# Normalising row blocks on GpSimd instead of VectorE in a four-layer attention kernel

## The chip, the cores and the metric

The kernel runs on one core of a Trainium2 chip. The metric is the device time of one execution in microseconds; of before there are three runs, 420.8 to 422.5, median 421.62. The five engines of the core work through queues of their own: PE (TensorE, matrix products), DVE (VectorE), ACT (ScalarE), POOL (GpSimd) and SP (SyncE, here only a queue of DMAs). Each engine takes its instructions in the order in which they stand, and waits on semaphores for those of the others.

## The reference

Four residual blocks over x of 2048 rows and 512 columns in bf16, with 32 heads of 16 columns; A and B each have one set of weights that is used twice.

```python
def _A_ref(x, wqkv, wo):                       # linear attention
    q, k, v = split(x @ wqkv)
    phi = lambda t: jnp.where(t > 0, t + 1, jnp.exp(t)) + 1e-6
    pq, pk = phi(q), phi(k)
    kv = jnp.einsum("bhsd,bhse->bhde", pk, v)  # a sum over all rows
    z = jnp.einsum("bhsd->bhd", pk)
    ...
    return merge(num / den) @ wo

def _B_ref(x, wqkv, wo):                       # softmax over a window of 256 rows
    ...

x = x + _A_ref(_layernorm(x), A_wqkv, A_wo)
x = x + _B_ref(_layernorm(x), B_wqkv, B_wo)
x = x + _A_ref(_layernorm(x), A_wqkv, A_wo)
x = x + _B_ref(_layernorm(x), B_wqkv, B_wo)
```

`_layernorm` takes the mean and variance of each row, subtracts the mean and divides by the root of the variance plus 1e-5. It has no weights. The kernel calls the last step, `(x - mean) * rstd`, on one block of 128 rows a normalising.

## The kernel before, in words

The 2048 rows are 16 blocks of 128, one row on each partition. x stays in SBUF throughout (`xres`, 16 tiles of 128 x 512 bf16). There are four normalisings per block, 64 in all:

- `1.ln`: before the keys and values of the first A layer. These are summed over all blocks (`kv`), so nothing that needs the sum starts before the last block.
- `2.b.ln`: before the first B layer. In segment 2 a block runs through the rest of the first A layer (`a_q`, `a_out`, `wo`, which updates `xres`), then through B (`b_qkv`, `b_attn`).
- `2k.ln`: before the keys and values of the second A layer, a block at a time as B finishes it; again they are summed over all blocks, in `kvacc`.
- `3.b.ln`: before the second B layer, in segment 3, which is as segment 2 with the output at the end.

One normalising is five operations (`ln`, L809 on): `st` and `ag` on DVE (L814, L815: statistics, mean and variance), `ae` on DVE (L817: adds 1e-5), `rs` on POOL (L818: to the power -0.5, one element per row), `xn` (L820: the normalised block, 128 x 512, from SBUF to SBUF). Then `xT` transposes the block: by a DMA that SP issues (L828), or for a few blocks by PE (L835) and a copy. The projections of PE read `xT`.

What else the text speaks of: phi of q and k is an exponential on ACT (L879), a clamp on DVE (`E`, L880) and an addition on DVE (L883; L885 for some). The attention of B is scores on PE (L1007, L1056), exponentials on ACT of 128 x 1024 (L1035, L1077: `pH`, `pF`), masks on DVE that multiply in SBUF (L1043, L1095), products with the values on PE (L1113, L1125), division on DVE (L1135, L1137). The values reach their place through a copy (`vt`, L845) and DMAs that POOL issues (`vd`, L981, four a block). Copies out of PSUM (`qc`, `kb`, `vc`, and others) may stand on ACT or on DVE.

The order of the work is written out as a list: `graph` records 2764 operations, each with the engines that can run it and a cost for each, and `ORDER` is a list of their numbers in the order in which they are issued. A mark behind a number (`445'`) takes the second engine of the operation; figures behind a colon name the buffers. `_Sched.schedule` walks this list; what it puts on one engine stays in that order on the chip, and `emit` sets the waits. The costs only give the walk its times; the chip doesn't see them.

Of the kernel before, what the change touches and what calls it, by code (L numbers as in the profile page):

```python
# [9 lines left out]
ALU = mybir.AluOpType  # L10
# [337 lines left out]
658' 671 626 627 672 673 902:6 907:2 684 903 986:0.4.1 987 988 919 449:0 904 955 905:3 881:1 906:3 882:3 883 921:0.6.0 922 923 908 909 685 686:2 687:1 450:5  # L348
884 1407 960:3.0.3 451 961 910:2 911 677:2.1.5 678 912:2 989 962 1408 924 1409 452 474:6.0 475 476 488 477 478:2 479:3 937:3 938 679 933:0.4.1 934 935 674:2.1
675 700 701 1410 932 939 940:1 720 964:0.6.2 702 703 965 966 688:5.0 689 690 691 1411:3 936 942:4 1412:0 941:1 489:0.3 490 943 501 676' 1021:2.6.2 1022 944  # L350
1023 704:0 491 492 493:0 494:1 705:3 967 692:5.2 693 945:2 946 947:0 680 963 721 694' 956:0.2.0 957 958 954 480:4 481 482 644 645 662 1418:7.1 995:0.5.4 996
997 722:1 723:2 1419 1420' 990 913:4 914 915 968:0.2.5 969 970 495:7 496 713:6.2.0 714 715 959 503 497 504:0.0 505 999:4.2.1 1000 1001 972:7 971 977:6 506 973
507 508:3 1056:0.4.0 1057 1058 1024 736 737 974 975:1 738 976:2 978 979 991:0.2.0 992 980:3 981 1421 1422 1423 998 710:7.3 711 712' 993 706:6.1 707 708' 709'
1030:0.4.3 681 716 1031 1032 695:3.1.1 696 994 948:2 1002 1003:0.6.2 697' 1004 949 950 1435 509:3 982:2 510:5 983:4 984 1005 1006 663 1034:0.2.5 1035 985 1036
511 1012:7 512 772 1436 1437 739 1438 740:2 741:4 1060 1007:6 1008 1439:3 1440:2 1424 1449 1450 1091:0.4.1 1092 754 1093 513:3.12.1 514 515 1013 1014 1009
1010:2 1451 517 1011:0 1026:0.4.0 1027 1028 728:2.0 1015:0 1016 1413:3.1.0 1414 1415 729 755 1425:0 1426:1 698 1037 1065:0.6.1 1066 730' 1416 1417 1067
731:5.0.3 732 724:4.2 733 725 1038:0.2.2 1039 1040 1441:7.0.2 1446:6.0 1447 1442 1029 1025 1033 1042:5 1443 1069:0.2.4 1070 1071 726' 1095 1043 727'
1427:4.4.3 1428 1429 699 1452 1448' 1453:1 1041 1047:6 1044 1126:0.2.2 1127 756 1444 1445 1068 746:7.1 747 1017:1 1045:1 1454:5 1046:1 1128 1430 1431 1048
1094 1061:0.4.0 1062 1063 1049 748' 1050:3 1051 757 1052:0 758:2 759:0 1018:3 1019 1100:0.6.3 1101 1102 1020 1465 1466 1467 1460:2.4 773 774 1455:5.3.0 1456
1073:0.3.5 1103 1461 1074 1457 1462 1432:7.3 742:6.3 1433 743 1075 775 1072 1059 1064 1077:2 1078 744 1458 1459 1104:0.4.2 1105 1106 1076 1434' 1079 1082:3  # L360
1083 745' 1080:2 1081:3 516 717 1161:0.6.0 1162 1163 1084 1085:0 764:2.2 765 1086 518 1087:2 766' 1096:0.4.0 1097 1098 1130 749:3.1.2 750 767:2.2.4 776:3 1107
1165 1135:0.6.1 1136 751' 1137 768 769' 1053:5 777:3 1054 1108:0.3.4 1099 1055 1479 760:2.4 761 762' 1468 1109 1110 1111 734 1112:7 1139:0.5.5 1140 1141 1113
1114 763' 1115:1 770 1469:0 1117:4 1118 1116:2 752 1196:0.2.1 519:5.3 1129 520 1197 521 522 1198 523:0 524:3 1119 1120:2 543:7.13.2 544 545 1480 1121 547
1088:1 1199 1131:2.5.0 1142 1089 1090 782:4.3 783 1164 1493 1132 1133 1134 528:7.14.3 1138 1170:0.2.3 1171 784' 1172 529 530 532 778:6.5 779 780' 781' 525:5
526 1143:0.2.2 753 1144 1145 527 790 791 735 1147:4 1148 792 1122:1 1494 1149 1150:0 1146 1151:1 1174:0.6.4 1175 793 1176 794:1 546 1470:3 1476:5.2 1477
1471:3.2.0 1478' 1177 1472 1473 1474 1475 1152:4 1153 1231:0.6.2 1232 1233 1481 531 1482 1154 1155:1 1156 1123:5 533 1124 1166:0.2.0 1125 1507 1173 558:4.15.1
# [72 lines left out]
class _Kernel:  # L439
# [369 lines left out]
    def ln(self, n, t, ring, dma=True):  # L809
        s = self.s  # L810
        x = self.xres[t]
# [7 lines left out]
        xn = self.r_xn.buf()  # L819
# [549 lines left out]
```

## Time and profile before

| | before |
|---|---|
| median of three runs | 421.62 us |
| lowest, highest | 420.8, 422.5 us |
| the profiled execution's own time | 422.47 us |
| its span in the profile | 421.1 us |
| PE, DVE, ACT, POOL busy | 392.3, 382.3, 383.6, 106.0 us |
| normalisings (L820), all on DVE | 64, 25.8 us |

Busy times are unions of the profiled durations. A duration on DVE or ACT includes the run-out of the instruction, in which the next one can already start. A row of a group reads: line, engine, operation, tiles written and read, shape and type, count, then busy us, mean ns of one, idle us of the engine just before them and what ended it. In the chain that ended last the columns are the start, the length booked on the chain, engine, tile and line.

### The profile page before, as it was taken

The numbers are of one execution on the slowest core, as the hardware profiler recorded it, in microseconds if no ns is written. First come the engines' busy times: TensorE is split into PE (matmuls) and PEld (weight loads), VectorE is DVE, ScalarE is ACT, GpSimd is POOL, SyncE is SP. The second block draws the span as 40 slices with busy tenths as digits, with TensorE's granted clock in tenths as the row PEclk, the third lists the DMA queues.
The fourth block names the chain that finished last, engine by engine and source line by source line (L and its number), as shares of the span: only waits on it lengthen the run. The fifth ranks groups of instructions, "written<-read, shape, count | busy, mean of one in ns | idle before, by whom it ended". The sixth has DMA issues, their size and how long they took to land.

```text
span 421.1 us, 18887 instructions
## 1 busy us (share of the span) xinstructions
PE 392.3 (93%) x8330; PEld 284.2 (67%) x8404; DVE 382.3 (91%) x1003; ACT 383.6 (91%) x496; POOL 106.0 (25%) x202
## 2 busy tenths in 40 slices
PE   7999989999999899998999999998999899988997
PEld 3655766776766676767586667676767667666675
DVE  7999899999999899998999899999999999978774
ACT  4888679999999999999899767899999999999995
POOL 2230024225232231423131100332322212605200
PEclk9999999999999999999999999999999999999999
DMA  8334426314252130523141201324415422406143
GB/s 265 112 64 138 128 55 126 66 41 99 41 68 43 38 67 16 85 41 59 39 80 22 48 9 39 70 48 68 79 34 80 60 52 33 90 16 117 43 103 92
DMA packets 75720, 29.22 MB, mean 69 GB/s; under 512 B 65264, under 2 KB 73584, under 8 KB 75632
## 3 DMA queue, kind: packets, MB, share of 16 engines
q1 hardware_dynamic: 70336, 22.36, 26.4%
q0 software_dynamic: 4096, 4.46, 5.7%
q8 instruction: 68, 1.11, 1.1%
q10 hardware_dynamic: 1200, 1.11, 0.9%
q14 instruction: 20, 0.16, 0.1%
HBM read 6.29 MB, written 2.10 MB: 20 GB/s over the span
## 4 chain that ended last, share of the span: by engine, by line
PE 42%; ACT 33%; DVE 18%; issue 3%; DMA 3%; POOL 0%; DVEq 0%
ACT pF L1077 23%; PE ps L858 16%; PE ps L870 8%; ACT pH L1035 6%; PE ps L1125 6%; PE ps L1056 5%; PE ps L1113 3%; DVE stats L814 2%; DVE o L954 2%; ACT kbd L971 2%; DMA w_Av<-in_A_wqkv_dram 2%; DVE pF L1095 1%; DVE xres L893 1%; PE ps L916 1%; PE ps L1007 1%
## 5 line engine op out<-in xcount | busy, mean ns | idle before, releaser
L1077 ACT ACTIVATE pF<-ps 128x1024 bf16<-128x1024 f32 x240 | 229.4, 1085 | 4.4 <-PE ps L1056 2.6
L818 POOL TENSOR_TENSOR rstd<-mv,const 128x1 f32<-128x1 f32 x64 | 39.1, 617 | 241.6 <-DVE mv L817 238.6
L981 POOL DMA_DIRECT2D vbd<-vt x128 | 67.1, 532 | 48.2 <-DVE vt L845 30.6
L1035 ACT ACTIVATE pH<-ps 128x1024 bf16<-128x1024 f32 (+1 forms) x64 | 60.3, 1022 | 3.5 <-PE ps L1007 3.2
L1125 PE MATMUL ps<-vbd,pF 128*128 128x34 bf16 x1856 | 60.2, 178 | 2.4 <-issue 2.4
L1125 PEld LDWEIGHTS ps<-vbd,pF 128*128 128x128 bf16 x1856 | 53.3, 96 | 5.5 <-issue 2.7
L1056 PE MATMUL ps<-qT,kbd 32*128 32x128 bf16 x1920 | 48.5, 216 | 5.0 <-ACT pF L1077 2.1
L1095 DVE TENSOR_TENSOR pF<-pF,const 128x512 bf16<-128x512 bf16 (+2 forms) x116 | 46.6, 415 | 3.6 <-ACT pF L1077 3.5
L879 ACT ACTIVATE E<-ps 128x512 bf16<-128x512 f32 x64 | 40.1, 630 | 9.8 <-PE ps L870 6.4
L814 DVE BATCH_NORM_STATS2 stats<-xres 128x6 f32<-128x512 bf16 x64 | 44.0, 689 | 2.0 <-DMA xres<-in_A_x_dram 1.1
L1056 PEld LDWEIGHTS ps<-qT,kbd 32*128 32x128 bf16 x1920 | 28.5, 92 | 22.6 <-ACT pF L1077 9.6
L1043 DVE TENSOR_TENSOR pH<-pH,const 128x1024 bf16<-128x1024 bf16 (+1 forms) x64 | 41.1, 649 | 0.0
L870 PE MATMUL ps<-xT,w_Bq 128*128 128x128 bf16 x512 | 35.5, 219 | 1.0 <-ACT pF L1077 0.7
L870 PE MATMUL ps<-xT,w_Bk 128*128 128x128 bf16 x512 | 35.6, 219 | 0.6 <-ACT pF L1077 0.4
L1113 PEld LDWEIGHTS ps<-vbd,pH 128*128 128x128 bf16 x928 | 29.0, 96 | 8.3 <-issue 2.2
L870 PE MATMUL ps<-xTa,w_Aq 128*128 128x128 bf16 x512 | 34.2, 219 | 0.3 <-DVE pq L883 0.2
L858 PE MATMUL ps<-w_Ak,xTa 128*128 128x512 bf16 (+2 forms) x121 | 32.3, 372 | 1.6 <-issue 0.8
L858 PE MATMUL ps<-w_Av,xTa 128*128 128x512 bf16 (+1 forms) x128 | 32.7, 371 | 1.1 <-issue 0.5
L1113 PE MATMUL ps<-vbd,pH 128*128 128x34 bf16 x928 | 32.7, 178 | 0.9 <-DVE kbd L971 0.3
L858 PE MATMUL ps<-w_Ao,oT 128*128 128x512 bf16 (+2 forms) x119 | 29.4, 354 | 4.2 <-issue 1.6
L870 PEld LDWEIGHTS ps<-xT,w_Bk 128*128 128x128 bf16 x512 | 29.8, 98 | 5.0 <-issue 0.9
L870 PEld LDWEIGHTS ps<-xT,w_Bq 128*128 128x128 bf16 x512 | 29.5, 98 | 5.3 <-issue 2.0
(96 smaller groups left out, 625.6 us busy)
## 6 DMA issues: line engine op xcount, KB each, us to landing
vbd<-vt POOLq DMA_DIRECT2D x128, 34.0 KB, 2.4
xres<-in_A_x_dram SPq DMA_DIRECT2D x16, 128.0 KB, 5.7
out_dram<-xres SPq DMA_DIRECT2D x15, 128.0 KB, 2.3
oT<-o SPq DMA_TRANSPOSE x60, 2.8
w_Ak<-in_A_wqkv_dram ACTq DMA_DIRECT2D x1, 512.0 KB, 5.4
w_Av<-in_A_wqkv_dram ACTq DMA_DIRECT2D x1, 512.0 KB, 6.9
w_Aq<-in_A_wqkv_dram SPq DMA_DIRECT2D x1, 512.0 KB, 7.0
w_Ao<-in_A_wo_dram SPq DMA_DIRECT2D x1, 512.0 KB, 3.9
```

The costliest lines, as they stand in the source:

```text
L814: s.op(n + ".st", {"DVE": 0.595}, lambda e, en: e.bn_stats(a_st, x.h[:]), reads=[x], writes=[st])
L858: i = e.matmul(g.h[:, a:b], xT.h[:, kt, :], w.h[:, kt, a:b], start=(kt == 0), stop=(kt == 3), skip_group_check=True)
L870: i = e.matmul(g.h[:, f * P:(f + 1) * P], w.h[:, kt, f * P:(f + 1) * P], xT.h[:, kt, :], start=(f == 0 and kt == 0), stop=(kt == 3), skip_ ...
L879: s.op(n + ".e", {"ACT": _act_cost(512)}, lambda e, en: e.activation(E.h[:], g.h, ACT.Exp, bias=0.0), reads=[g], writes=[E])
L981: return [e.dma_start(vbd.h[64 * a:64 * a + 64, j, a], vt.h[64 * j:64 * j + 64, a]) for j in range(2)]
L1035: return e.activation(d, c, ACT.Exp, bias=0.0, scale=DH ** -0.5)
L1043: return e.tensor_tensor(v, v, tr, ALU.mult)
L1056: i = e.matmul(ss[r // 2].h[:, r % 2, k * P:k * P + P], kbds[fj[m] // 2].h[32 * r:32 * r + 32, f, fj[m] % 2, :], qT.h[32 * r:32 * r + 32, ...
L1077: s.op("e%d%d" % (u, g), {"ACT": _act_cost(1024)}, lambda e, en, S=ss[g], pb=pb, g=g: e.activation(pb.h[:, 2 * g:2 * g + 2, :], S.h, ACT.E ...
L1095: return e.tensor_tensor(v, v, tr, ALU.mult)
L1113: i = e.matmul(U.h[:, c:c + 34], pH.h[:, 4 * r + f, 64 * a:64 * a + P], vbds[j // 2].h[:, j % 2, :, 4 * f + r, :], start=first[0], stop=Tr ...
L1125: i = e.matmul(U.h[:, c:c + 34], pFs[at[f, m][0]].h[:, r, at[f, m][1] * P:at[f, m][1] * P + P], vbds[fj[m] // 2].h[:, fj[m] % 2, :, 4 * f ...
```

## The change

`xn` may run on POOL, and the order list is replaced by another. In the new list 51 of the 64 `xn` carry the mark for POOL; 13 stay on DVE.

```diff
 def ln(self, n, t, ring, dma=True):
...
         s.op(n + ".rs", {"POOL": 0.53}, lambda e, en: e.tensor_tensor(a_rs, v, self.half.h[:], ALU.pow), reads=[mv, self.half], writes=[rs])
         xn = self.r_xn.buf()
-        s.op(n + ".xn", {"DVE": 0.32}, lambda e, en: e.tensor_scalar(xn.h[:], x.h[:], self.mv[:, t, 0:1], a_rs, op0=ALU.subtract, op1=ALU.mult),
+        s.op(n + ".xn", {"DVE": 0.32, "POOL": 0.7}, lambda e, en: e.tensor_scalar(xn.h[:], x.h[:], self.mv[:, t, 0:1], a_rs, op0=ALU.subtract, op1=ALU.mult),
              reads=[x, mv, rs], writes=[xn], new=[xn])
...
 ORDER = """
-37 4 0 3 6 7 1 8 9 2 68 61:7 69 70 5 67 71 72:0 73:6.0 62 38 66 85 86 87 10 39 40 88 41 42 43 44 45 46 11 33 12 13 20 47 89:1 22 74 75:7.0.0 76 90:6.1 81:5.0
+1 67 3 2 4 0 6 7 8 9 37 68 5 69 70 39 40 61:7 38 66 41 71 72:0 73:6.0 85 86 87 42 43 44 45 46 33 10 74 62 75:7.0.0 76 11 12 13 88 22 89:1 90:6.1 25 91 32 102
...
```

Counted in the two lists:

| | before | after |
|---|---|---|
| `xn` on DVE: `1.ln`, `2.b.ln`, `2k.ln`, `3.b.ln` | 16, 16, 16, 16 | 3, 4, 4, 2 |
| `xn` on POOL | 0, 0, 0, 0 | 13, 12, 12, 14 |
| `kb` of segments 2 and 3 on ACT, DVE | 25, 39 | 26, 38 |
| `qc` on ACT, DVE | 8, 24 | 7, 25 |
| `vc` of segments 2 and 3 on ACT, DVE | 9, 23 | 8, 24 |
| `vc` of `1` on ACT, DVE | 10, 6 | 9, 7 |
| `vc` of `2k` on ACT, DVE | 6, 10 | 10, 6 |
| `zc` of the last block on ACT, DVE | 3, 1 | 2, 2 |

All other operations stay on their engines. Their order changes on every engine; which block's transposition runs on PE or by DMA does not.

More of the change, by code (lines that the diff above doesn't have):

```diff
@@ L348 @@
[L348 to L355, printed above, removed]
@@ new lines @@
+352 353 109:6.2.1 110 186 205 206':1 187 188 126:7.3.2 127 130 116 149:3.3 150 157':2 173 174':3 189 26 219 52 367 111 128 266 190':0 220 53 282 283 117
+143:2.4.3 129 158:1.5 18 159 144 145 131 366 221 368 222:2 267 268 151 269 207:6 132:7.4 133 112 270':1 147 101 166:1.5 167 284 408:0.3.2 54 55 250 251 113
+114 252 253 134 168' 409 412 214:6.6 215 410 208:7.5.0 209 212 210 285 146 160:3.6.1 161 162 148 234 235 236 27 164 28 163 211 213 165 175:7 176:2.7.3 177 118
+180 182:7.7 135 183 178 191:8 192:3.0.0 193 223:9 29 23 152 230:2.0 198:1.1 231 194 411 196 413 179 232 314 315 316 181 271:10 278:0.2 279 272:3.1.1 273 274
@@ new lines @@
+1407 988 921:0.3.0 922 923 908 1408 449:1 450:7 451 452 960:0.5.3 961 686':1 687:0 924 909 910:1 911 912:2 962 677:4.1.5 678 679 474:0.0 475 476 937:7 477
+478:3 479:3 1409 933:2.5.1 934 935 989 963 1410 1411':3 938 674:4.1 939 940:3 941:0 936 964:0.2.2 965 675 489:5.2 490 688:7.0 689 966 676' 942:4 491 492 943
+493:1 700 701 690 691 702 1021:0.2.2 944 480:5 481 1022 1023 945:1 946 703 704:0 956:0.6.0 957 482 955 692:4.2 693 913:5 995:0.2.4 694' 958 996 914 1412:1
+1418:4.6 1419 736 737 738 968:0.6.5 997 969 915 1420' 959 494:0 495:5 496 504:2.0 505 705:3 990 970 713:4.0.0 714 715 497 999:0.6.1 1000 1001 644 645 972:5
@@ new lines @@
+973 506 971 967 680 681 977:4 974 507 508:2 1056:0.2.0 754 1057 1058 739 740':2 1421 978 755 979 706:7.1 975:3 976:3 980:2 981 991:0.5.0 992 1002 707 708' 993
+710:4.3 711 709' 1030:0.2.3 1422 1031 1032 721 722':1 712' 947:1 948:6 949 756 950 1435 695:7.2.1 1003:0.4.2 1004 982:3 1005 696 697' 509:2 983:6 984
+1034:0.2.5 1035 510:7 1036 1423 1424 1436 511 1437 994 1438 998 1007:5 1006 1012:4 1013 723:2 985 512 772 1449 1037 1450 1091:0.2.1 1014 1015:1 1439':3 1440:0
+513:7.12.1 514 1008 1092 1024 1451 1009 1025 1093 515 1010:0 516 517 716 717 1026:0.2.1 1027 698 1425':0 728:6.0 729 1413:7.5.2 1011:1 1016 1017:0 1426:2
@@ new lines @@
+1065:0.4.2 1452 1453:1 1028 741:4 1414 1066 1067 730' 724:3.2 725 731:6.1.3 732 1415 1038:0.4.0 1059 1454:5 1446:2.0 1447 1095 733 726' 727' 773 1416 1029
+1417 1441:3.2.3 1448' 2718 1039 1040 1442 1443 1069:0.6.4 1070 1071 699 1033 1041 1444 1445 757 1427:2.6.0 1428 1042:5 1047:4 1060 1043 1044 1045:3 1046:0 734
+1429 1126:0.6.2 1127 1048 1430 1128 1049 1431 1050:2 1051 1052:1 1072 746:5.1 1061:0.2.1 747 1062 1063 1018:4 1019 518 748' 1100:0.6.3 1101 1020 1465 1130
+1432:5.5 1102 1064 1068 758':3 759:1 1433 1434 1460:4.4 1461 1073:0.2.5 1462' 742:7.3 774 743 744' 745' 1074 1077:6 1075 1076 1104:0.4.0 1078 1079 1080:0 1105
@@ new lines @@
+1106 1455:7.4.2 1456 1082:3 1129 1466 1467 1468 1469':0 1081:3 1457 1458 1161:0.4.0 1162 1163 1459 764:2.2 1107 1083 735 1084 1096:0.6.1 1097 1098 1085:1 1086
+765 766' 1103 749:5.0.2 750 751' 1135:0.3.2 1136 1137 767:2.2.4 1087:3 1094 768 1053:7 769' 1108:0.5.4 1109 1054 1099 760:4.4 1110 761 1055 762' 1139:0.2.5
+1140 1141 1111 775 1112:7 763' 1113 1114 1115:3 1117:6 519:0.2 1116:2 520 521 522 523:1 1196:4.2.1 543:7.13.3 544 770 1479 1197 1199 1198 547 545 1118
+1131:0.4.1 1119 1164 1120:0 1121 1088:3 1132 1133 1138 1089 1090 1493 776':2 1480 777:3 778:7.5 779 528:6.14.0 780 781' 529 532 1165 530 782:5.3 1170:0.2.3
@@ new lines @@
+783 784' 1494 1134 524:2 525:7 526 527 790 1171 1172 1495 791 792 1142 1470:3 531 533 1143:0.4.0 1144 1145 1146 752 753 793 794:1 1471:6.1.1 1472 1147:7
+1174:0.2.4 1175 1176 1148 1149 1150:1 1476:5.2 1477 1473 1152:4 1153 1478 1231:0.2.2 1232 1233 1474 1475 1154 1151:0 1155:3 1156 1122:0 1123:5 546 1124 1125
+1507 1496 1497':3 1166:0.6.1 785:4.1.5 786 787' 1167 1168 1508 558:5.15.2 559 562 560 534:0.2 535 536 537 538:3 1205:2.6.2 795:0 548 1169 1206 1207 796:4.0
+797 798' 800:5.0 1173 1178:0.2.5 1179 1180 801 803:7.0.1 1481 1177 799' 1182:6 1183 1184 1200 1209:0.2.0 1210 1211 804 1181 1187:4 1188 1185:0 1186:1 802'
@@ new lines @@
+856' 1662:3.2.2 1663 1664 1666 1321 1349:4.6.5 1350 1317 1521:1.0 1304 852' 853' 1322:2 861 1323 1324 1340 1522 1695 1348 1351 1352 1341:0.4.1 1697 1325:3
+1326:2 1327:3 1328 1329 1342 1343 1353:0.6.3 1330:2 1331 1344 1354 1543:2.4.3 1297:0 1298:5 1569':0 1299 1300 1581 1785 1355 1371:0.3.0 1372 1374 1373 1544
+1545 843 1357:7 1582 1562:6.5 1356 1358 1563 1564 1359 1583 1584 1585':2 1360:0 1361:1 1380:0.4.0 1381 1382 1332:1 1546 1547 1375 1665 1362:3 1363 1364 1365:1
+1366 1384:0.6.2 1385 1737:2.4.1 1333:5 1667 1386 1334 1383 1335 1595 1596 1376:0.3.1 1377 1378 1597 1379 1738 1557:7.5.3 1558 1570:11 1571:6.6.2 1572 1559
@@ new lines @@
+1941 2253:7 2254 2271 2249:0.4.4 2250 2251 1766 2255 2256:2 1973:3.1.0 2257:3 1974 2273:0.6.5 2274 2275 1955:2.2.2 1997 1998 1975' 2252 2222:5 2223 2224
+2277:0.3.0 2278 2279 1956 2272 2225:1 2226 2284 2258:7 2259 1957' 1982':3 2304:0.5.2 1983:0 1988:2.1 1989 1778:3 2305 2260 2306 2276 2014 1990' 1984:4.3
+2261:3 2317:0.2.3 2318 2319 2262 2280 1788:5.0 1789 1790 1791 1792:1 1779:7 1780 1781 1985 2320 1986 1987 1803:0.2 1804 1999 1805 65 2227:0 1806 2285:5.2.2
+2286 1958 1807:2 2228:7 2229 2230 2287 1991:4.0.3 1992 2308 1993' 2309:0.5.4 2310 2311 1959 2289:7 2288 2195:1 2000':1 2290 2291 2292:1 2293:0 2313:0.2.5 2314
@@ new lines @@
+2565:0.6.1 2566 2567 2142 2143 2336:5 2548 2528 2559 2337 2564 2338 2605:0.3.3 2549:0 2606 2607 2144':1 2145:4 2541:7 2542 2592:5.0.1 2593 2594 2543 2544:1
+2117:3.2.5 2545:1 2568 2550 2118 2551:3 2572 2443:2 2573:4.6.2 2574 2119' 2577:2 2578 2579 2580:3 2581:2 2575 2597:0.4.5 2138 2598 2599 2595 2128:3.5 2129
+2130' 2153:2.0.1 2139 2601:0.6.4 2602 2603 2154 2146:5.0 2147 2576 2131' 2628:0.3.2 2629 2630 2155' 2148' 2149' 2480:2 2481 2482 2641:6.0.1 2582:5 2642 2643
+2120 2121 2632 2600 2583 2604 2584 2585:2 2586 2609:2.6.0 2610 2611 2150:4.2 2151 2596 2152' 2162':0 2163:0 2171:5.1.2 2633:0.2.2 2634 2608 2635 2172 2173'
@@ L431 @@
+2612 2613:4 2614 2637:6.0.5 2638 2587:0 2639 2615 2616:1 2617:0 2444:5 2445 2446 2644 2447 2664:2.6.0 2168:4.3 2169 2636 2665 2666 2170' 2631 2618:5
[4 rows of a table added]
+2714:0.2 2716 2715:2 2725:2 2717 2730:5 2731 2732 2726:7.2 2733:1 2734 2727' 2696:6 2748:1 2749 2735:5.0 2750 2697 2743 2744:7.1 2720:4 2719:0 2339 2736 2728
+2737 2751:0 2729 2752 2753:5.3 2591 2745' 2738 2747 2754 2746 2755 2757 2756 2760 2761 2698 2699 2758 2627 2762 2759 2763
 """
```

92 lines of the change are left out of this document (34 added, 58 removed), and 63 rows, old and new, of the table ORDER.

## The prediction

> **What bounds the kernel now.** I read the page first (busy time of each engine, then the chain that ended last), then the busy time by stretch, then the chain through the middle.
>
> ```profile
> span 421.1 us, 18887 instructions
> ...
> PE 392.3 (93%) x8330; PEld 284.2 (67%) x8404; DVE 382.3 (91%) x1003; ACT 383.6 (91%) x496; POOL 106.0 (25%) x202
> ...
> PE 42%; ACT 33%; DVE 18%; issue 3%; DMA 3%; POOL 0%; DVEq 0%
> ```
>
> Three engines are over 90% busy and GpSimd (POOL) is at 25%. So no single engine bounds the span; each stretch has its own limit. The next view gives busy us (and instruction counts) by stretch. I set the cuts from the chain: 45.5 is where the first key-value sum is in, 60.5 the first attention exponential of the second segment, 225 roughly its last tile, 267 the first exponential of the third segment, 404.8 the last but for the tail.
>
> ```profile
> core 0: us, PE busy (x) PEld busy (x) DVE busy (x) ACT busy (x) POOL busy (x), PEclk, DMA share, GB/s
> 0.00:45.50 45.50, 43.02 (x309) 23.98 (x314) 38.75 (x135) 34.10 (x61) 10.01 (x26) 1.00 0.53 157
> 45.50:60.50 15.00, 13.17 (x179) 9.96 (x178) 14.12 (x44) 11.09 (x19) 2.19 (x4) 1.00 0.20 39
> 60.50:106.00 45.50, 42.46 (x925) 31.71 (x938) 43.65 (x113) 44.59 (x58) 16.67 (x31) 1.00 0.41 83
> 106.00:225.00 119.00, 112.27 (x2628) 83.57 (x2654) 111.10 (x277) 114.46 (x140) 31.26 (x56) 1.00 0.30 51
> 225.00:267.00 42.00, 40.21 (x646) 28.88 (x653) 39.53 (x110) 31.65 (x51) 5.71 (x10) 1.00 0.18 34
> 267.00:404.80 137.80, 127.43 (x3293) 95.89 (x3309) 125.80 (x305) 136.07 (x155) 40.18 (x76) 1.00 0.36 63
> 404.80:421.10 16.30, 13.72 (x383) 10.18 (x385) 9.36 (x26) 11.62 (x16) 0.00 (x0) 1.00 0.38 93
> ```
>
> Read ACT's column against the length of each stretch. In 60.5 to 106 ACT idles 0.91 us and in 267 to 404.8 only 1.73 us: these 183 us are ACT's, and less work on VectorE (DVE) can hardly shorten them. In 106 to 225 it idles 4.54 us, with DVE and PE nearly as full. In 225 to 267 ACT idles 10.35 us; there DVE leads the chain:
>
> ```profile
> 258.41 0.71 DVE stats L814
> ...
> 260.48 0.59 DVE o L954
> 261.07 0.32 DVE xn L820
> 261.39 0.61 DVE xres L893
> ```
>
> The step that moves is this `xn L820`. Between 0 and 45.5 PE is full (43.02 of 45.5); in the tail no row block is left to normalise.
>
> **What the change takes off DVE.**
>
> ```profile
> L820 DVE TENSOR_SCALAR xn<-xres,mv,rstd 128x512 bf16<-128x512 bf16 x64 | 25.8, 405 | 2.4 <-POOL rstd L818 2.2
> ...
> 209.05 0.41 DVE L820 TENSOR_SCALAR xn<-xres,mv,rstd 128x512 bf16<-128x512 bf16 x1
> 209.38 0.69 DVE L845 CAST vt<-ps 128x512 bf16<-128x512 f32 x1
> ```
>
> One takes 405 ns, but the next operation starts 0.33 us after it (209.05 to 209.38), and the chain books 0.32 us for it too. What DVE gains is 51 x 0.32 = 16.3 us, not 51 x 0.405. It also loses 51 of 64 parts of the 2.2 us in which it sat waiting for GpSimd's `rstd`, 1.8 us; half of that on the path is 0.8 when rounded down. Where those 16.3 us lie matters more. The same view for L820 alone counts how many normalisings each stretch holds:
>
> ```profile
> 0.00:45.50 45.50, 6.40 (x16) 1.00 0.53 157
> 45.50:60.50 15.00, 1.19 (x3) 1.00 0.20 39
> 60.50:106.00 45.50, 2.81 (x7) 1.00 0.41 83
> 106.00:225.00 119.00, 7.35 (x18) 1.00 0.30 51
> 225.00:267.00 42.00, 2.42 (x6) 1.00 0.18 34
> 267.00:404.80 137.80, 5.66 (x14) 1.00 0.36 63
> ```
>
> In the new order list DVE keeps the blocks 0, 1, 9 of the first segment; of the second segment's attention blocks 3, 7, 12, 15; of the next key-value pass 3, 7, 13, 15; of the third segment 1 and 13. Counted into the stretches above in the old order, 13, 3, 5, 14, 3 and 13 move. So only 3 leave the stretch where DVE leads most clearly (2k blocks 12 and 14, third-segment block 0), and 31 leave stretches that PE or ACT fills.
>
> The gain by stretch, without costs: 0 to 45.5, nothing, PE hides it (if that cover were gone, 13 x 0.32 = 4.2 us at most). 45.5 to 60.5, where DVE is 14.12 of 15 busy: 3 x 0.32 = 1.0 us off the queue, less the longer way of the first block (below), 0.2. 60.5 to 106 and 267 to 404.8: at most ACT's idle time, 0.9 and 1.7; I take 0.3 each. 106 to 225: 14 x 0.32 = 4.5 us, about ACT's 4.54 idle; PE, 94% busy, also holds ACT up, so half, 2.0. 225 to 267: 3 x 0.32 = 1.0. That is 3.8 us, and 4.6 with the waits.
>
> The rest of the relayout moves little work: counted in the two order lists, ACT takes four more value copies of the second key-value pass and one more key mask, DVE takes one q copy, two value copies and a small copy of the tail. PE changes between its two kinds of matmul 304 times in both. The sequence itself is a cost I can't see: bounded by the idle time it could recover or lose in 225 to 267, I keep 4 us either way for the range and 0 for the sum.
>
> **What it adds on GpSimd.** No row of before shows this operation there. The nearest:
>
> ```profile
> L981 POOL DMA_DIRECT2D vbd<-vt x128 | 67.1, 532 | 48.2 <-DVE vt L845 30.6 <-ACT vt L845 11.3 <-DVE E L880 3.8
> L818 POOL TENSOR_TENSOR rstd<-mv,const 128x1 f32<-128x1 f32 x64 | 39.1, 617 | 241.6 <-DVE mv L817 238.6 <-DVE const L723 1.5 <-DVE mv L815 1.4
> L730 POOL IOTA const<- 128x128 int32 x1 | 0.2, 225 | 0.0
> L729 POOL IOTA const<- 128x4 int32 x1 | 0.1, 127 | 0.0
> ```
>
> The two iotas differ by 98 ns for 124 elements, 0.79 ns each. From below: 127 ns and 508 more elements, 0.53 us. From above: the 0.617 us of a one-element operation plus 511 x 0.79, 1.02 us. I take 0.75, the middle. GpSimd then has 106.0 + 51 x 0.75 = 144 us of work in 421: not a bound. Queued behind a normalising are the `vbd` DMA issues (532 ns each, two or four in a row) and the next `rstd`; who waits for it is SP's queue of DMA transposes, in which those of `oT` stand behind a late `xT`. Compared with DVE a block is ready 0.75 - 0.32 = 0.43 us later, less one hop between engines. Most blocks are normalised well ahead of their projection, so I charge it only on the first blocks of the second and third segments (both on GpSimd): 0.4 each, the first already taken off above, the second inside the cost below.
>
> **The cost on DVE.** GpSimd and DVE hinder each other already:
>
> ```profile
> 189.88 1.28 DVE L1043 TENSOR_TENSOR pH<-pH,const 128x1024 bf16<-128x1024 bf16 x2
> ...
> 190.05 2.05 POOL L818 TENSOR_TENSOR rstd<-mv,const 128x1 f32<-128x1 f32 x2 [8.73 <-DVE mv L817]
> ...
> L818 POOL TENSOR_TENSOR rstd<-mv,const x64: 537/558/1537, 4.1 to 378.7; 128x1 f32<-128x1 f32 x64
> ```
>
> Minimum, median and longest of `rstd` are 537, 558 and 1537 ns. The longest begins inside two mask multiplications with both inputs in SBUF and ends about 0.4 us after them, so GpSimd waited for DVE. The reverse can't be seen here: `rstd` has one element per lane and holds nothing for long. A normalising moves 512 each way. The operations that could be held:
>
> ```profile
> L1095 DVE TENSOR_TENSOR pF<-pF,const 128x512 bf16<-128x512 bf16 (+2 forms) x116 | 46.6, 415 | 3.6 <-ACT pF L1077 3.5
> ...
> L1043 DVE TENSOR_TENSOR pH<-pH,const 128x1024 bf16<-128x1024 bf16 (+1 forms) x64 | 41.1, 649 | 0.0
> ...
> L880 DVE TENSOR_SCALAR E<-E 128x512 bf16<-128x512 bf16 x64 | 18.0, 283 | 1.2 <-ACT E L879 1.1
> ...
> L883 DVE TENSOR_TENSOR pq<-pq,E 128x512 bf16<-128x512 bf16 x32 | 13.2, 414 | 0.4
> ...
> L883 DVE TENSOR_TENSOR pk<-pk,E 128x512 bf16<-128x512 bf16 x16 | 6.6, 422 | 0.9 <-ACT pk L882 0.7
> ```
>
> The five rows are 292 operations in 421 us, 0.69 per us. If GpSimd holds them off for about 0.5 us, 0.35 of the holds meet one and cost half a hold: 0.09 us each, 51 x 0.09 = 4.5 us against 16.3 gained. From below 0 (no hold at all); from above a hold of the whole 1.02 us meets 0.70 and costs 0.36, 18.3 us. I take 4.5: an operation of 0.75 us moves its elements in the part beyond a fixed start, as the iotas' 127 of 225 ns do. Of it 0.6 falls on the path in 106 to 225 (half of 14 x 0.09), 0.3 in the middle and 0.3 at the head; the third segment's first block may cost 0.3 more, the rest of its 0.4 hidden by DVE's own queue. Costs: 1.5.
>
> The Trainium skill (SBUF — State Buffer, Who interferes with whom) states that a DVE operation in a two-port mode, or with two SBUF inputs beside a GpSimd operation that reads SBUF, and GpSimd shut each other out, and whoever is first keeps the shared port pair for the whole instruction. The lengthened `rstd` agrees as far as GpSimd's wait goes; the reverse no run here shows. By that rule a hold lasts the whole 0.75 us, costs 51 x 0.19 = 9.9 us of DVE, and the costs above would be about 2.9 instead of 1.5.
>
> **The sum.** 422.47 us is the profiled execution's own time (span 421.1 and 1.4 around it), 0.85 above the median of 421.62. Gain 4.6 less 1.5 is 3.1: 419.4 for that execution, 418.5 against the median, 0.7% faster. About 0.5% (2.1 us) is what a measurement of this kernel can tell from no change.
>
> **The rivals.**
> *All of it counts.* If the new order turns the freed DVE time into ACT's work, ACT's idle time in 106 to 225 goes (4.5) and a third of the 10.35 in 225 to 267 (3.5): 421.6 - 8 = 413.6. For it: DVE is at 93% or more in both. Against: ACT's work is unchanged and only 3 blocks leave the second.
> *Nothing moves.* ACT and PE fill 183 + 45.5 us as they did, the middle's chain passes to `xres`, `stats`, `o`, and what is gained is given to holds: 421.6, within 2.
> *Slower: the holds outweigh the relief.* If one GpSimd normalising takes over about 1 us, and holds the operations above for all of it, DVE loses more per block than the 0.32 us it saved; that is the point where it turns. At 1.3 us a hold meets one in 0.69 x 1.3 = 0.90 of the cases and costs 0.58: 51 x 0.58 = 30 us lost against 16.3. In 106 to 225 the 14 blocks lose 14 x 0.26 = 3.6 net, half on the path, 1.8; the 6 blocks of the middle and the head lose 1.6; blocks ready 1 us later at the heads of two segments add 2.0: 421.6 + 5.4 = 427.0. With the stall near its turning point the lateness alone is left: 423.6. For it: 1537 ns against 537 shows that the two engines do collide, and every wait of GpSimd for DVE lengthens the block's way too. Against: no DVE row here shows the reverse, so the length is a guess between 0.53 and 1.02.
>
> The Trainium skill (GPSIMD Engine Reference, Engine selection) keeps elementwise work on DVE, calling GpSimd about twice as slow with two inputs and near line rate with one; no row here has such an operation.
>
> **How the numbers follow.** Forecast 0.38, all counts 0.14, nothing moves 0.10, slower 0.38. The forecast lies not far from the bound: of its 0.38 I count 0.30 as faster by over 0.5% (below 419.5) and 0.08 as within; nothing moves adds 0.10 to that. Faster 0.44, within 0.18, slower 0.38. The forecast's own range is 416.5 to 421. The range for 8 in 10 reaches from 412.5, a little beyond the best case, to 428, a little beyond the slower one.
>
> **What would show it.** Right: L820 on POOL at 0.6 to 1.0 us, x51; DVE busy about 358 to 366; mean durations of L1095 and L1043 within 5% of 415 and 649 and no new idle time before them; ACT's idle time in the second segment down by some 2 us and from 267 on unchanged. Wrong: L820 on POOL over 1.2 us; L1095, L1043, L880 longer or with new gaps; PE's transposes or projections waiting for `xT`; or the time between the last exponential of the second segment and the first of the third longer than now.

## The result and the profile after

| | before | after |
|---|---|---|
| median | 421.29 us (4 runs) | 440.06 us (4 runs) |
| lowest, highest | 420.8, 422.5 | 439.8, 441.44 |
| span of the profiled execution | 421.1 us | 438.5 us |

The ratio is 1.0435, 95% interval 1.0414 to 1.0456: 18.8 us slower, where I had forecast 418.5 with a range of 412.5 to 428. From the page of after, in this order: busy time, GpSimd's row of the forty slices, the chain that ended last, and the group that moved.

```profile
span 438.5 us, 18891 instructions
...
PE 396.8 (90%) x8332; PEld 284.2 (65%) x8408; DVE 376.8 (86%) x951; ACT 384.3 (88%) x497; POOL 215.6 (49%) x253
...
POOL 3989236555857072385336220484357355436300
...
ACT 39%; PE 29%; DVE 13%; POOL 11%; DMA 5%; issue 2%; SPq 0%; DVEq 0%; POOLq 0%
...
L820 POOL TENSOR_SCALAR xn<-xres,mv,rstd 128x512 bf16<-128x512 bf16 x51 | 109.8, 2153 | 4.3 <-POOL rstd L818 0.5
```

One normalising takes GpSimd 2.15 us in the mean, against 0.75 in the forecast and 1.02 as its upper bound. GpSimd's total, 49%, looks harmless; its slices do not: in `3989` it is busy for at least 80%, mostly over 90%, of the second to fourth slice (11 to 44 us). It holds 11% of the chain, where it held 0%.

The busy times by stretch, with the columns of the prediction's table. The first cut is the same time as in before's, 45.5 us; the others are at the same events (the first attention exponential of segment 2 at 70.5; near the last block's at 240.9; the first of segment 3 at 283.4; its last block's at about 422):

```profile
0.00:45.50 45.50, 35.67 (x234) 18.47 (x238) 33.59 (x105) 26.53 (x48) 36.00 (x39) 0.96 0.39 108
45.50:70.50 25.00, 22.16 (x251) 15.44 (x251) 22.15 (x63) 18.72 (x31) 9.03 (x8) 1.00 0.48 134
70.50:118.00 47.50, 43.57 (x968) 32.02 (x978) 43.94 (x108) 44.76 (x58) 29.53 (x38) 1.00 0.39 68
118.00:240.90 122.90, 114.42 (x2631) 83.40 (x2636) 105.68 (x260) 114.59 (x142) 60.52 (x71) 0.99 0.29 50
240.90:283.40 42.50, 40.24 (x614) 28.70 (x620) 38.83 (x106) 30.70 (x51) 10.25 (x11) 1.00 0.17 35
283.40:422.00 138.60, 127.14 (x3286) 95.86 (x3310) 123.55 (x289) 137.45 (x158) 70.26 (x90) 1.00 0.36 61
```

Take ACT's idle time, the length less ACT's column. The head (first two rows) has 25.25 us of it, where before had 15.31: 9.9 lost. The second segment (next two) has 11.05 against 5.45: 5.6 lost. The middle loses 1.4, the third segment gains 0.6. ACT's work is 0.7 us more and its idle time in the tail 0.3 longer; together 17.4, the whole difference of the spans. In the first row PE does 35.67 us of work instead of 43.02 while GpSimd does 36.00 instead of 10.01: GpSimd has taken PE's place as the limit of the head. The chain of after shows it there (start, length booked, engine, tile, line):

```profile
12.00 0.57 POOL rstd L818
12.67 2.08 POOL xn L820
14.75 0.54 POOL rstd L818
15.38 2.21 POOL xn L820
17.59 1.05 POOL rstd L818 x2
18.73 4.13 POOL xn L820 x2
22.87 0.54 POOL rstd L818
23.50 2.39 POOL xn L820
25.89 0.54 POOL rstd L818
26.52 2.08 POOL xn L820
28.60 0.54 POOL rstd L818
...
65.61 2.08 POOL xn L820
67.69 0.54 POOL rstd L818
68.32 2.09 POOL xn L820
70.43 4.10 DMA xT<-xn
```

From 12.0 to 29.1 there is nothing but normalisings and `rstd`, one behind the other, and the same again ahead of the second segment. The waits of SP's queue agree; a DMA transpose waits there for its block (us in total, times, longest):

```profile
SPq L828 <- POOL xn L820: 96.1, 27, 10.7
SPq L828 <- DVE o L1137: 36.3, 8, 8.3
SPq L828 <- POOL rstd L818: 25.4, 10, 6.8
```

96.1 us in 27 waits for a normalising on GpSimd; in before it was 32.7 in 9 for one on VectorE. These are waits of a queue and not time lost, but they tell whom the blocks keep waiting.

The granted clock changes too. The column PEclk, 1.00 throughout in before, has 0.96 in the first row and 0.99 in the fourth: PE was granted half its clock in two stretches of 3.41 us, from 31.9 and from 137.8 us. Ahead of each lie 3.41 us in which PE was busy for 0.11 and 1.40 us, so they come right behind its waiting. My estimate from these figures is at most half of 6.8 us, 3.4 of the 17.4, and that only if PE set the pace throughout.

### The profile page after: what moved, and what is told of

It reads as the page before. It is cut to its first block, busy times and chain, and to the rows that moved or that the text cites. A ratio compares the mean times of both kernels' runs of the same rounds, so it can differ in the third digit from the quotient of the medians.

```text
span 438.5 us, 18891 instructions
## 1 busy us (share of the span) xinstructions
PE 396.8 (90%) x8332; PEld 284.2 (65%) x8408; DVE 376.8 (86%) x951; ACT 384.3 (88%) x497; POOL 215.6 (49%) x253
## 4 chain that ended last, share of the span: by engine, by line
ACT 39%; PE 29%; DVE 13%; POOL 11%; DMA 5%; issue 2%; SPq 0%; DVEq 0%; POOLq 0%
ACT pF L1077 29%; PE ps L858 14%; ACT pH L1035 7%; POOL xn L820 7%; PE ps L870 5%; PE ps L1125 3%; PE ps L1056 3%; POOL rstd L818 2%; POOL vbd L981 2%; DMA xT<-xn 2%; PE ps L1113 2%; DMA xres<-in_A_x_dram 2%; DVE o L954 2%; ACT kbd L971 1%; DVE stats L814 1%
## 5 line engine op out<-in xcount | busy, mean ns | idle before, releaser
L820 POOL TENSOR_SCALAR xn<-xres,mv,rstd 128x512 bf16<-128x512 bf16 x51 | 109.8, 2153 | 4.3 <-POOL rstd L818 0.5
L981 POOL DMA_DIRECT2D vbd<-vt x128 | 69.0, 550 | 32.6 <-DVE vt L845 29.9
L1035 ACT ACTIVATE pH<-ps 128x1024 bf16<-128x1024 f32 (+1 forms) x64 | 60.5, 1020 | 2.8 <-PE ps L1007 2.6
L1095 DVE TENSOR_TENSOR pF<-pF,const 128x512 bf16<-128x512 bf16 (+2 forms) x116 | 47.8, 421 | 2.4 <-ACT pF L1077 2.1
L879 ACT ACTIVATE E<-ps 128x512 bf16<-128x512 f32 x64 | 38.8, 619 | 11.4 <-PE ps L858 8.7
L858 PE MATMUL ps<-w_Ak,xTa 128*128 128x512 bf16 (+2 forms) x127 | 35.1, 396 | 5.8 <-DVE mv L817 3.5
L858 PE MATMUL ps<-w_Bv,xT 128*128 128x512 bf16 (+2 forms) x127 | 29.9, 346 | 5.2 <-DVE qT L845 2.0
L858 PE MATMUL ps<-w_Bo,oT 128*128 128x512 bf16 (+2 forms) x127 | 29.0, 344 | 4.4 <-ACT pF L1077 1.5
```

Source lines behind the costliest of these rows:

```text
L820: s.op(n + ".xn", {"DVE": 0.32, "POOL": 0.7}, lambda e, en: e.tensor_scalar(xn.h[:], x.h[:], self.mv[:, t, 0:1], a_rs, op0=ALU.subtract, o ...
L858: i = e.matmul(g.h[:, a:b], xT.h[:, kt, :], w.h[:, kt, a:b], start=(kt == 0), stop=(kt == 3), skip_group_check=True)
L981: return [e.dma_start(vbd.h[64 * a:64 * a + 64, j, a], vt.h[64 * j:64 * j + 64, a]) for j in range(2)]
L1035: return e.activation(d, c, ACT.Exp, bias=0.0, scale=DH ** -0.5)
L1095: return e.tensor_tensor(v, v, tr, ALU.mult)
```

## The experiments

The two theories after the result: **length** (GpSimd works its queue in order, and an operation of 2.08 us delays the block, and what stands behind it), and **holds** (GpSimd keeps VectorE from SBUF, the forecast's slower rival). Beside them: is the new order itself worth something, and is the relief of VectorE?

**How the cost depends on the form of the operation.** The normalisings on GpSimd take six forms, chosen by the block's number modulo 6; five of the six are variants, of which four leave out the subtraction or put constants in place of the row's values:

```diff
+            if k == 1: return e.tensor_scalar(o, a, 0.01, 0.25, op0=ALU.subtract, op1=ALU.mult)
+            if k == 2: return e.tensor_scalar(o, a, a_rs, None, op0=ALU.mult)
+            if k == 3: ...   # two halves of 256 columns
+            if k == 4: return e.tensor_tensor(o, a, a_rs.to_broadcast([P, D]), ALU.mult)
+            if k == 5: return e.tensor_scalar(o, a, 0.25, None, op0=ALU.mult)
             return e.tensor_scalar(o, a, m, a_rs, op0=ALU.subtract, op1=ALU.mult)
```

> The changed kernel with the 51 GpSimd normalisings in six forms by block number modulo 6: 0 as in the kernel (two scalars read per partition), 1 two immediate scalars, 2 one scalar per partition and one operation, 3 the kernel's form in two halves of 256 columns, 4 a tensor_tensor with the scale broadcast, 5 one immediate and one operation. Forms 1, 2, 4 and 5 leave out or replace part of the normalising. This measures what sets the 2.08 us. If it is the elements, each half of form 3 takes about 1.1 us and the others stay near 2; if it is the scalars read per partition, form 1 and 5 fall to about 0.75; if it is the two operations, 2 and 5 fall to about half. Holds says nothing here.

By line of that kernel, ns minimum, median, longest: the form of the change (L835), immediates (L825), one operation with a scalar per partition (L827) and with an immediate (L834), the first half (L829), the tensor_tensor (L832).

```profile
L835 POOL TENSOR_SCALAR xn<-xres,mv,rstd x10: 2079/2084/2182, 20.6 to 365.8; 128x512 bf16<-128x512 bf16 x10
L825 POOL TENSOR_SCALAR xn<-xres x6: 1925/1935/2043, 23.3 to 329.3; 128x512 bf16<-128x512 bf16 x6
L827 POOL TENSOR_SCALAR xn<-xres,rstd x12: 1567/1576/2114, 9.3 to 394.6; 128x512 bf16<-128x512 bf16 x12
L834 POOL TENSOR_SCALAR xn<-xres x8: 1504/1608/2047, 18.5 to 362.6; 128x512 bf16<-128x512 bf16 x8
L829 POOL TENSOR_SCALAR xn<-xres,mv,rstd x7: 1228/1353/1656, 11.5 to 402.0; 128x256 bf16<-128x256 bf16 x7
L832 POOL TENSOR_TENSOR xn<-xres,rstd x8: 1041/1042/1103, 14.6 to 354.1; 128x512 bf16<-128x512 bf16 x8
```

The minimum of 2079 ns belongs to the operation itself, not to a collision. From 256 to 512 columns it grows by 851 ns (1228 to 2079): 3.3 ns per element, and about 0.38 us fixed. The one time of this kernel was 441.25 us. The tensor_tensor with two inputs costs half; that gave the next three kernels.

**Shorter operations in after's place.** The 51 on GpSimd become one tensor_tensor by `rstd`, over 512, 256 or 128 columns (in the narrow two, two blocks of the first segment keep 512). The subtraction of the mean is left out, and in the narrow two the other columns:

```diff
+            if en == "POOL":
+                return e.tensor_tensor(o[:, 0:w], a[:, 0:w], a_rs.to_broadcast([P, w]), ALU.mult)   # w = 512, 256, 128
```

> The changed kernel, its list and its 51 places on GpSimd untouched, but each of the 51 is one tensor_tensor that only multiplies by rstd (the subtraction of the mean is left out): 1.04 us in the run of six forms, against 2.08. Length: on a line from the forecast (418.5 at 0.75) to the result (440.1 at 2.08), 16.2 us per us, it expects 423, within 4. Holds, if GpSimd reads for as long as before (0.62 us), expects 432 or more. Order, the list being bad whatever the length, expects 435 or more.

> As the run before it, but the multiplication covers 256 of 512 columns (the rest keeps old values; two early blocks are full): 0.80 us by the two known lengths, 0.56 for one element and 1.04 for 512, so about the length that the forecast took. Length expects 416 to 422, and with it the forecast's gain would be right for its own length. Holds expects 424 or more, order 435 or more.

> As the run before it with 128 columns, about 0.68 us. Length expects 414 to 421. If it isn't faster than before although GpSimd's part is this short, then the relief of 16 us of DVE is worth nothing in this kernel, and the forecast's gain was wrong as well as its price. Order expects 435 or more.

The lengths of the stretches here and below are those of the profiled execution: head, to the first attention exponential of segment 2; second, from there to that of its last block; middle, to the first of segment 3; third, to that of its last block. "Lengthened" sums what VectorE's operations took beyond before's median for the same operation and shape, counting those that took some 50 ns more or longer.

| | op, us | ratio to before (interval) | head | second | middle | third | lengthened, us |
|---|---|---|---|---|---|---|---|
| before | | 1 | 60.5 | 165.1 | 41.6 | 136.7 | |
| after | 2.08 | 1.0435 (1.0414 to 1.0456) | 70.5 | 170.4 | 42.5 | 137.7 | 6.8 |
| tt_full | 1.04 | 1.0287 (1.0254 to 1.032) | 63.9 | 168.7 | 42.0 | 141.7 | 18.4 |
| tt_half | 0.61 | 1.0106 (1.0064 to 1.0147) | 61.0 | 167.2 | 41.4 | 138.1 | 5.5 |
| tt_quarter | 0.40 | 1.0048 (1.0026 to 1.007) | 60.0 | 166.4 | 41.4 | 137.0 | 2.4 |

The head and the second segment go with the length of the operation; the third goes with the holds. (Part of tt_full's third segment may be the clock: its profile has one half-clock stretch of 3.41 us, from 298.7.) The holds are nearly three times as large with the tensor_tensor of 1.04 us as with the change's operation of 2.08, yet the kernel is faster than after. The page of tt_full has the masks at 476 ns in the mean, before's at 415:

```profile
L1103 DVE TENSOR_TENSOR pF<-pF,const 128x512 bf16<-128x512 bf16 (+2 forms) x116 | 54.1, 476 | 1.8 <-ACT pF L1085 1.6
```

With 0.61 us, less than the 0.7 that the change writes down as GpSimd's cost and than my 0.75, the kernel is still 1.1% slower than before.

**The order and the engine apart.** order_only keeps after's list and puts all `xn` back on VectorE; engine_only keeps before's list and moves the same 51:

```diff
-            o.eng, cost = list(o.engs.items())[word.endswith("'")]
+            ...[word.endswith("'") and not o.name.endswith(".xn")]                    # order_only
+            ...[word.endswith("'") or (o.idx in MOVED and not self.mark)]             # engine_only
```

> The new order list with all 64 normalisings on DVE. Three theories for the 18.8 us that the change lost. Length: a normalising on GpSimd takes 2.08 us (51 rows of the profile after), not 0.75, and blocks come late where nothing is queued ahead of them. Holds: what costs is DVE standing still at the ports that GpSimd keeps (some 6 us by the lengthened DVE rows). Order: the new sequence is worse by itself. Length and holds both expect 417 to 425 here, order expects 434 or more. If it is below 419.5, the new sequence is a better one that only GpSimd spoils.

> The order list of before with the same 51 normalisings on GpSimd. Length expects the loss of the change or more, 438 to 448, since nothing in this list was arranged for it. Holds expects 424 to 430. Order expects 419 to 425.

order_only: 491.34 us, ratio 1.1637 (1.1591 to 1.1682), which all theories missed. I take it that the list's places for `xn` are meant for GpSimd's queue and come late in VectorE's; the waits of the DMA transposes for `xn` fit that, but don't show that it is the whole loss:

```profile
SPq L828 <- DVE xn L820: 59.7, 8, 15.2
```

VectorE itself waits for `rstd` only 5.3 us in all, and the granted clock is 0.951, so why this kernel loses 69 us stays open, and it doesn't tell what the order is worth.

engine_only: 444.54 us, 1.0523 (1.0489 to 1.0558), head 70.5, second 176.0, third 136.7. So the engine change alone costs 22.7 us, and the new list takes back some 0.9%, about 4 us; the gain lies in the second segment (176.0 to 170.4).

**One segment at a time.** In after's list the 13 of the first segment go back to VectorE (head_back), or they alone stay on GpSimd (head_only); in before's list those 13 (head13), the 24 up to the second sum (second24) or the 14 of the third segment (third14) move alone.

```diff
+            ... and o.name != "1.ln.xn"                                               # head_back
+            ... and (o.name == "1.ln.xn" or not o.name.endswith(".xn"))               # head_only
+MOVED = {...}     # 13, 24 or 14 of the 51: head13, second24, third14
```

> The changed kernel with the 13 normalisings of the first segment back on DVE, 38 left on GpSimd. ACT's idle time up to its first attention exponential was 10.5 us longer after the change than before. Length, with the first segment's GpSimd queue (13 x 2.08 + 16 x 0.56 = 36 us) as the largest loss, expects about 440 - 10 = 428 to 432. Holds expects 434 to 438, since of the lengthened DVE rows about 4 of 6 us lie before 50 us. Order expects 438 to 441.

> The changed kernel with only the 13 normalisings of the first segment on GpSimd, the other 38 back on DVE. Length expects 421 + 10 = 429 to 433, the complement of the run before it. Holds expects 424 to 428. Order expects 438 to 441.

> The order list of before, only the 13 normalisings of the first segment on GpSimd. With all 51 on GpSimd in this list ACT's idle time before its first attention exponential grew by 10.0 us (22.4 to 32.4). Length expects that alone: 430 to 434. Holds, with some 4 us of lengthened DVE rows there against 4.2 us taken off DVE, expects 420 to 424.

> The order list of before, only the 24 normalisings of the second segment (12 before attention, 12 before the next keys and values) on GpSimd. With all 51, ACT's idle time between the first exponentials of its first and last block grew by 10.9 us, and by 1.1 us from there to the third segment. Length expects 431 to 435: a block is 1.7 us later where transposes and projections follow it at once. Holds expects 418 to 423, since few DVE rows are lengthened here against 24 x 0.32 taken off.

> The order list of before, only 14 normalisings of the third segment on GpSimd. ACT is busy nearly throughout there, and with all 51 its idle time in that stretch did not grow. Length expects 420 to 424, the first block 1.7 us later at most. Holds expects the same, 420 to 424. If it is below 420, the relief of DVE counts where blocks have slack.

head_back, 440.19 us (1.0434, 1.0404 to 1.0464), lies where the order theory had it and not where length or holds had. head_only, 488.43 (1.1579, 1.1554 to 1.1604), missed all three. Both take operations out of GpSimd's places in after's list, as order_only does, so they don't tell the loss by GpSimd from the loss by the list. The runs in before's list do:

| | median, us | ratio (interval) | head | second | third |
|---|---|---|---|---|---|
| head13 | 430.02 | 1.0203 (1.017 to 1.0236) | 68.3 | 164.1 | 136.7 |
| second24 | 433.93 | 1.0302 (1.0261 to 1.0342) | 60.7 | 171.1 | 136.7 |
| third14 | 422.48 | 1.0016 (0.9999 to 1.0033) | 59.7 | 164.6 | 136.6 |

The parts cost 8.3, 12.2 and 0.7 us; the sum, 21.2, is nearly the 22.7 of all 51. The four executions of second24 lie apart: the profiled one, at full clock, took 429.11, the other three, at 0.992, 433.25 to 435.87, so part of its 12.2 us seems to come with the lower clock. The same operation that costs 0.6 us apiece in the head costs nothing that can be told from noise in the third segment, where ACT is 99% busy.

**Only blocks with time to spare.** slack9 moves nine that before's trace shows finished 2.4 to 17 us ahead of their next user (before's list, `MOVED` of nine).

> The order list of before with 9 normalisings on GpSimd in full, those after which the trace of before shows 2.4 to 17 us between their end and the issue of their transposition (second segment's attention block 7, next keys and values 4, 5, 7, 8, third segment 6, 8, 9, 14). Length expects no loss where blocks have slack, and a gain of at most 9 x 0.32: 419 to 422. Holds expects the same. Below 419.5 it beats both kernels.

426.14 us, 1.0118 (1.009 to 1.0146); the second segment 168.8 instead of 165.1, the rest unchanged. GpSimd's timeline of it, and of before at the same place:

```profile
189.38 1.54 POOL L819 TENSOR_TENSOR rstd<-mv,const 128x1 f32<-128x1 f32 x1 [8.74 <-DVE mv L818]
191.03 2.07 POOL L821 TENSOR_SCALAR xn<-xres,mv,rstd 128x512 bf16<-128x512 bf16 x1
193.08 0.55 POOL L819 TENSOR_TENSOR rstd<-mv,const 128x1 f32<-128x1 f32 x1
193.63 2.07 POOL L821 TENSOR_SCALAR xn<-xres,mv,rstd 128x512 bf16<-128x512 bf16 x1
195.65 1.12 POOL L982 DMA_DIRECT2D vbd<-vt  x2
```

```profile
190.05 2.05 POOL L818 TENSOR_TENSOR rstd<-mv,const 128x1 f32<-128x1 f32 x2 [8.73 <-DVE mv L817]
192.07 1.25 POOL L981 DMA_DIRECT2D vbd<-vt  x2
```

Counted from the first `rstd`, the second `rstd` and the two `vbd` issues come 2 and 4 us later, though they belong to other blocks and other steps. What this costs can be followed from there. Two rows of slack9's waits:

```profile
DVE xn L821 <- POOL rstd L819: 4.9, 4, 3.0
PE ps L859 <- DVE o L1138: 3.5, 2, 3.2
```

The longest wait of each is one event. The second `rstd` ends at 193.63, behind another block's normalising; for it waits the normalising of a block that was not moved, on VectorE, which stands idle for 3.0 us; behind that stands the division `o` (L1138), for which PE stands idle for 3.2 us, until 195.0. In before PE waits 0.8 us at this place. Counted from the first `rstd`, PE goes on 2.4 us later than in before; from 194.3 to 197.7 it then has half its clock, and ACT's next exponential is 3.9 us late. The whole segment is 3.7 us longer. That spoke for the queue; the last pair of runs was made to separate it.

**The queue without the blocks, and the relief without the queue.** ghost51 leaves all normalisings on VectorE and gives GpSimd a like operation that nobody reads, behind the `rstd` of the 51 blocks. relief51 moves nothing, and 49 of them work on 32 columns on VectorE.

```diff
+            i = e.tensor_tensor(a_rs, v, self.half.h[:], ALU.pow)
+            if ghost: e.tensor_scalar(scratch, constant, self.half.h[:], self.one.h[:], ...)   # 128 x 480; ghost51
+            return i
...
+        w = 32 if ... else D                                                            # relief51
+        ... e.tensor_scalar(xn.h[:, 0:w], x.h[:, 0:w], self.mv[:, t, 0:1], a_rs, ...)
```

> Before's list, all 64 normalisings in full on VectorE; behind the rstd of each of the 51 blocks GpSimd also runs a tensor_scalar of 128 x 480 with two scalars per partition on constants, about 2.0 us, whose output nobody reads. So no block waits for its own normalising on GpSimd; only what stands behind it in GpSimd's queue (the next blocks' rstd, the vbd issues) comes late, and VectorE may be held. Theory now (the queue does it): most of the 22.7 us that the same 51 cost on GpSimd comes back, 435 to 443, the head longer by 6 to 10 and the second segment by 6 to 11, the third not. Rival (a block's own lateness does it): only holds are left, 421 to 425, head and second segment within 2 of before.

> Before's list, nothing on GpSimd; 49 of the 51 normalisings that the change moves stay on VectorE but work on 32 of 512 columns (the other columns keep older data), so VectorE is relieved of most of 49 x 0.32 = 15.7 us and nothing is paid for it. If the relief is worth what I forecast (4.6 us): 416.5 to 417.5. If it is worth nothing that can be measured, as the quarter-width run suggests, because ACT and PE fill the span: 420 to 421.5. Theory now: the second.

ghost51: 442.25 us, 1.0484 (1.0463 to 1.0505), head 72.8, second 171.5, middle 41.9, third 137.7. The loss is back, with every block normalised on VectorE. Its chain through the head, and what VectorE waits for:

```profile
14.24 0.56 POOL rstd L826
14.80 1.96 POOL const L828
16.76 0.53 POOL rstd L826
17.29 1.96 POOL const L828
```

```profile
DVE xn L833 <- POOL rstd L826: 12.8, 13, 1.8
```

VectorE waits 12.8 us for `rstd`; in before 2.2. A block's own like operation comes only after its `rstd`, so what is ahead of a late `rstd` belongs to other blocks. The run is not a pure one: VectorE's operations were lengthened by 10.6 us, 7.6 of it its own `xn`, which now meet the GpSimd operation. VectorE's busy time grew by 4.3 us in the head (52.87 to 57.19), which is 12.3 longer, and by 3.8 in the second segment (155.34 to 159.10), which is 6.4 longer; so even if all of that growth reached the end, 8 us of the head are left for the queue. In the second segment 2.6 us are left; PE had 6.8 us at half clock there, from 207.9, right behind 3.41 us in which it was busy for 1.52, and by the estimate above that is worth up to 3.4 us.

relief51: 421.07 us against 421.58, ratio 0.9987 (0.9975 to 0.9998). The relief was smaller than I wrote: one of 32 columns still keeps the queue for 0.20 us in the median instead of 0.32, so 49 save 6.1 us of VectorE. Of those 0.1 to 1.1 us reach the end. No version beat before by the 0.5% that the prediction took as the least that can be told.

## Why the prediction was wrong, point by point

- **What bounds the kernel.** That no one engine does, and that ACT fills the third segment, held: 136.6 to 136.7 us in before, engine_only, head13, second24, third14 and slack9. That "PE hides" the head was the error of reading: PE hides VectorE there, but not a third engine that can become longer than PE. GpSimd's own sum for the head was never made. With the measured length it is 13 x 2.08 + 16 x 0.56 = 36 us of 45.5, which the stretch shows (36.00).
- **The length on GpSimd, the term that failed.** 0.75 us, bounds 0.53 and 1.02; measured 2.08. The nearest rows were an operation that only writes (the iotas) and one of a single element; neither reads 512 elements and computes two steps on each, which costs 3.3 ns per element and not 0.79. So the upper bound was no bound. "Not a bound", said of 144 us in 421, used an average over stretches of different kinds.
- **Lateness, 0.4 us on two blocks.** "Most blocks are normalised well ahead of their projection" was looked at for the block alone. The engine works in order, so each moved operation delays the `rstd` of later blocks and the `vbd` issues; the prediction named them as queued behind and charged them nothing. slack9 shows 1.2% from nine blocks with slack, ghost51 most of the loss with no block moved.
- **The holds, 4.5 us.** Right in size: 6.8 us in after, 4.9 in engine_only, less than VectorE's relief. They are not what made it slow. The minimum, median and longest of the addition of phi (L883) and the clamp (L880) in after; in before the longest were 426 and 302:

```profile
L883 DVE TENSOR_TENSOR pq<-pq,E x32: 360/418/876, 15.7 to 342.9; 128x512 bf16<-128x512 bf16 x32
L880 DVE TENSOR_SCALAR E<-E x64: 229/286/718, 11.0 to 332.9; 128x512 bf16<-128x512 bf16 x64
```

  One case in the timeline of after:

```profile
12.67 2.08 POOL L820 TENSOR_SCALAR xn<-xres,mv,rstd 128x512 bf16<-128x512 bf16 x1
...
12.84 0.87 DVE L883 TENSOR_TENSOR pk<-pk,E 128x512 bf16<-128x512 bf16 x1
13.63 0.28 DVE L880 TENSOR_SCALAR E<-E 128x512 bf16<-128x512 bf16 x1
```

  The addition ends 1.04 us after the normalising began and the clamp runs at its usual 0.28 us, both inside its 2.08 us. The Trainium skill (SBUF — State Buffer, Who interferes with whom) has the pair of ports held for the whole instruction; by that rule neither could have. The hold covers a part of this operation only. In after's trace 19 operations of VectorE that begin in the first 0.6 us of a normalising are lengthened by over 50 ns; 15 of them end 0.62 to 0.64 us plus their usual length after its start (the addition of 0.42 us at 1.04). Four clamps that begin 1.57 to 1.84 us after it are held again, to 1.94 us plus their usual 0.285. With 0.62 us in place of 0.5 the forecast's way of counting gives 51 x 0.43 x 0.31 = 6.8 us, about what was measured; so its idea of a partial hold was right, though it had the operation at 0.75 us.
- **The gain, 4.6 us.** Too large. VectorE was relieved (382.3 to 376.8 us busy, with the holds in it), but 6.1 us of relief for nothing are worth 0.1 to 1.1 us; at the forecast's rate without the waits for `rstd`, which relief51 keeps (3.8 for 16.3), it would be 1.4. In tt_quarter the whole relief beside an operation of 0.40 us still ends 0.5% behind before. The 2.0 us in 106 to 225 were put on VectorE's account because ACT idled as long there as VectorE would be freed; that two times are equal doesn't make one the cause of the other.
- **The new order, 4 us either way and 0 for the sum.** Inside its bound: about 4 us back against engine_only, so after without it would have been slower still.
- **The slower rival (0.38).** Its sign came true. Its turning point, "about 1 us", did not: at 0.61 us the kernel is 1.1% slower than before, and at 0.40 us still 0.5%. Nor did its mechanism (holds for all of the length), and so its price of 5.4 us. Its share for lateness, 2.0 us, is the part that grew into the result. The signs that the prediction listed for "wrong" were the right ones: L820 on POOL over 1.2 us; PE's transposes waiting for `xT` or `xn`, as this row of after's waits shows:

```profile
PE ps L835 <- POOL xn L820: 4.1, 4, 1.4
```

What stays open: how the loss of the second segment divides between late blocks, `rstd`, `vbd` and the half-clock stretches that follow; the worth of the new order with `xn` on VectorE, and why order_only loses so much; and why the tensor_scalar takes twice as long as the tensor_tensor.

## What to carry to other kernels

Before work goes to an engine that looks idle, add up that engine's queue for each stretch, with the added work at a length measured for that very form of operation; where no trace shows the form, the range must allow several times the guess. On an engine that works in order, a long operation is paid by the short ones behind it: nine blocks with slack cost 5 us, most of it at one place, where the `rstd` of another block stood behind one of them and VectorE, then PE, waited for it. Relieving an engine that is 91% busy is worth little if the engines beside it are as full: here 6 us off VectorE gave at most 1.1.

## What the hardware showed that I had not expected

- On GpSimd a bf16 tensor_scalar of 128 x 512 with two operations takes 2.08 us, with one 1.50 to 1.61, with immediates instead of scalars per partition 1.93; a tensor_tensor with a broadcast second input, of the same shape, 1.04 us, and 0.61 and 0.40 for 256 and 128 columns. VectorE takes 0.41 for the first. The Trainium skill (GPSIMD Engine Reference, Engine selection) calls GpSimd roughly line rate with one input and about twice as slow as VectorE with two. Here the tensor_scalar, with one input, takes five times VectorE's 0.41; the tensor_tensor, with two, takes 2.5 times the 0.42 of VectorE's tensor_tensor of this shape (L883), which is nearer to the page.
- The faster form hinders VectorE more: 51 tensor_tensors of 1.04 us lengthened VectorE's operations by 18.4 us, 51 tensor_scalars of 2.08 us by 6.8. In tt_full's trace 20 of the 28 lengthened operations end 0.90 to 0.93 us plus their usual length after the start of the 1.04 us operation, so it holds VectorE for nearly all of its length, where the tensor_scalar does so for the first 0.62 us of 2.08.
- A wait of PE can be followed by a lower granted clock: the half-clock stretches of after, engine_only, slack9 and ghost51 (3.41 or 6.83 us each) each follow 3.41 us in which PE was busy for 0.1 to 1.5 us. Before has none; between 12 and 400 us PE is busy there for at least 2.4 us of any 3.41. A wait alone isn't always enough: second24's profile has one of 3.0 us at 201.7 and no half-clock stretch.
